# Big products of a slot put next to each other, dummy products in one group, a weight conversion tied to its place

## The chip, the cores and the metric

The kernel runs on one core of a Trainium2 chip. The metric is the device time of one execution in microseconds (us), less is better. Two kernels are compared by the medians of several executions on the same chip.

## The reference

Three computations follow each other. A recurrent attention over 768 steps for 4 batches of 8 heads of size 40, then an MLP with SiLU (320 to 2048 and back), then a gated MLP (320 to 1536 twice, a sigmoid on one, their product, and back to 320). Everything is float32.

```python
for t in range(S):                       # attention, S = 768
    y[:, :, t] = einsum('bhd,bhde->bhe', rt, state)
    Sa = einsum('bhde,bhe->bhd', state, at)
    state_decay = state * wt[:, :, None, :] - einsum('bhd,bhe->bhde', Sa, bt)
    state = state_decay + einsum('bhd,bhe->bhde', vt, kt)
...
h = x @ w_in;  g = h * (1.0 / (1.0 + np.exp(-h)));  x = g @ w_out          # first MLP
gate = 1.0 / (1.0 + np.exp(-(x @ w_gate)));  val = x @ w_val               # second MLP
out = gate * val @ w_out2
```

## The kernel before

The recurrence is cut into chunks of 32 steps. One chunk of one batch is a *slot*; there are 24 chunks times 4 batches, so 96 slots with attention work, and the first MLP trails the attention by 16 slots. A loop over `n` issues slot after slot, and an order written out as a string sets what stands behind what inside a slot: one string for the slots below 16 (`NL`), one for the others. Each letter is a short step on TensorE (PE), and most have a copy on ScalarE (ACT) or VectorE (DVE) behind them:

- `u` (`c_u`, tile `ps_u`), `v` (`c_ut`, `ps_ut`, "u's transpose"), `R` (`c_rhs` of the next slot, `ps_r`), `q` (`c_pu`, `ps_lp`), `t` (`c_st`, `ps_t`), `p` (`prep`, tile `wt`, then copied to `ks` and `yl`), `y` (`c_y`, `ps_y`), `s` (`c_s`, `ps_s`, the last link of a slot's state), `z` (`z_fix`, `ps_z`, odd slots up to 13 alone). All of these are small: 8 or 16 products, 16 to 40 columns wide. `ps_s` needs `ks` from `prep` and `sr` from `u`.
- `lb` (`e_sys`) builds the triangular systems of a later chunk, in about every second slot. DVE inverts them in short steps (`ztmp`, `zh`).
- The digits `0` to `3` call `mlp`. From slot 16 on, `0` and `1` are the two halves of the first MLP's up-projection (`m1_up`, tile `hp`, 8 products of 256 columns each) and `2` and `3` the two halves of the down-projection of the hidden block before (`m1_down`, tiles `acc`, 6 products of 320 columns each). Below slot 16 there is no MLP work yet, and each digit issues 4 *dummy* products with the identity instead (`warm(4, 2)`, tile `acc_w`, 256 columns); their result is never read.

The order on PE is fixed: `in_turn` makes a step follow the last product issued. The order on the other engines is decided by a scheduler that works ahead of time, except where `tc.issue_after` ties an instruction: `behind()` gives the instructions inside it a place behind the last copy to `yl` of `prep` and the last multiplication of `c_y` issued so far. Instructions without a tie may be put wherever the scheduler thinks an engine has room.

The weights arrive as 64-bit floats. `conv_load` starts the load (tile `cvr`), `conv_do` makes float32 of it (tile `cvt`: ACT lines 694 and 695, DVE lines 696 and 697, GpSimd line 698), and a float32 value is then split into a high and a low half. For the first MLP this runs inside `behind()` (`wtick`). For the second MLP `conv2` (lines 985 to 989) does it, without a tie. Its results lie in memory that the attention frees at its end, but `cvr` and `cvt` do not, so the first few conversions can begin long before.

Of the kernel before, what the change touches and what calls it, by code (L numbers as in the profile page):

```python
# [8 lines left out]
F32 = mybir.dt.float32  # L9
# [4 lines left out]
ALU = mybir.AluOpType  # L14
# [22 lines left out]
def kernel(  # L37
    ctx, tc, ins, wkab, rv, vn, w_in, w_out, w_gate, w_val, w_out2, out
):
    nc = tc.nc  # L40
# [145 lines left out]
    CW = 320  # L186
# [118 lines left out]
    NL = 16  # L305

    def in_turn():
        return tc.issue_after(last_op[0].ins) if now[0] >= 0 else nullcontext()
# [81 lines left out]
    def behind():  # L390

        g = ExitStack()
        for x in last_q.values():
            g.enter_context(tc.issue_after(x.ins))
        return g
# [79 lines left out]
    def warm(n, w=1):  # L475

        if not n:
            return
        ps = pa.tile([128, DM], F32, tag="acc0", name="acc_w")
        for _ in range(n):  # L480
            last_op[0] = nc.tensor.matmul(  # L481
                ps[:, :128 * w], identr,
                identr.unsqueeze(1).to_broadcast([128, w, 128]), start=True, stop=True,
            )
# [187 lines left out]
    def conv_load(rows, n, src, mp, cw):  # L672
        if wide:
            raw = mp.tile([128, cw, 2], I32, tag="cvr", name="cvr", bufs=4)
            t = raw.rearrange("p a b -> p (a b)")[:, :2 * n]
        else:
            raw = mp.tile([128, cw], F32, tag="cvt", name="cvt", bufs=2 + 1)
            t = raw[:, :n]
        r0 = 0
        for x in src if isinstance(src, tuple) else (src,):  # L680
            nc.sync.dma_start(t[r0:r0 + x.shape[0]], x)
            r0 += x.shape[0]
        return raw

    def conv_do(raw, rows, n, mp, cw):

        if not wide:
            return raw[:rows, :n]
        t = mp.tile([128, cw], F32, tag="cvt", name="cvt")[:rows, :n]
        lo, hi = raw[:rows, :n, 0], raw[:rows, :n, 1]  # L690
        ti = t.bitcast(I32)


        nc.scalar.mul(t, hi.bitcast(F32), 2.0 ** -112)
        nc.scalar.activation(lo, lo.bitcast(U32), AF.Copy, bias=2.0 ** 23, scale=2.0 ** -29)
        nc.vector.tensor_scalar(ti, ti, 3, None, op0=ALU.logical_shift_left)  # L696
        nc.vector.scalar_tensor_tensor(ti, hi, -0x80000000, ti, op0=ALU.bitwise_and, op1=ALU.bitwise_or)  # L697
        nc.gpsimd.tensor_tensor(ti, ti, lo, op=ALU.add)  # L698
        return t
# [34 lines left out]
    def wneed(p):  # L734

        f = min((p + 1) * max(1, NF1 // 8), NF1)
        o, n = 0, 0
        while o < FF1 and o < 128 * f:
            w = min(CW, FF1 - o)
            n += 3 + (NF1 if o + w == FF1 else (o + w) // 128) - o // 128  # L740
            o += w
        return n
# [33 lines left out]
    def defer(k, f):  # L776
        late.setdefault(now[0] + k, []).append(f)
# [7 lines left out]
    def hi_run(f, a):  # L785
        with behind(), tc.high_priority(offset=300):
            f(*a)
# [59 lines left out]
    if True:  # L847
# [12 lines left out]
        for x, t in enumerate(when):  # L860
# [7 lines left out]
            if stream[x] == e_units(gi)[-1]:  # L868
                i0 = t + 2
                i1 = min(gi * 8 - 4, i0 + 7)  # L870
                hi = lambda f: lambda *a: hi_run(f, a)
# [21 lines left out]

        def mlp(n, which):
            m = (n - 8 - 8)
            if m < 0:
                with in_turn():
                    warm(4, 2)
            if NP1 < 8 and m % 8 >= NP1:
                return  # L900
            if m < 0:
                return
            kb, p = divmod(m, 8)
            if kb >= NJ:
                return
            mm = kb * NP1 + p

            with tc.issue_after((last_op[0] if 1 else rhs_i[max(0, min(n, NS - 1) - [0, 0, 0, 0][which])]).ins):
                if which in (0, 1):
                    m1_up(mm, which)  # L910
                elif mm > 0:
                    m1_down(mm - 1, which - 2)

        for n in range(NS + 8 + 8):
            now[0] = n
            if 8 + 8 <= n < 16 + 8:
                while wpos[0] < min(wneed(n - 8 - 8), len(wsteps)) + LW:
                    wtick()
            for f in late.pop(n, ()):
                f()  # L920
            if n < NS and n not in rhs_i:
                c_rhs(n)
            for o in ['cuRqz0tp1vys23l', 'zcq01uv23tpRysl'][n >= NL]:
                if o in '0123':
                    mlp(n, int(o))
                turn = in_turn() if o in 'uvqptRsyz' else nullcontext()
                turn.__enter__()
                if o == 'R' and n + 1 < NS and n + 1 not in rhs_i:
                    c_rhs(n + 1)
                if o == 'z' and n % 2 == 0 and 0 < n < NS - 2:  # L930
                    z_load(n + 2)
                for x in range(2):
                    if o == 'zs'[x] and n % 2 == [1, 1][x]:
                        z_fix(n + 2 - [1, 1][x], x)
                if o == 'c' and n % 2 and n + 3 < NS:
                    c_load(n + 3)
                if o == 'l' and n % 2 == 0 and 0 < n and n + 2 < NS:
                    r_load(n + 2, 0)
                if o == 'l' and n % 2 and 1 < n and n + 1 < NS:
                    r_load(n + 1, 1)  # L940
                if o == 'u' and n < NS:
                    c_u(n)
                if o == 't' and 0 <= n - 3 < NS - NB:
                    c_st(n - 3)
                if o == 'q' and 0 <= n - 1 < NS:
                    c_pu(n - 1)
                if o == 's' and n < NS:
                    c_s(n)
                if o == 'v' and n < NS:
                    c_ut(n)  # L950
                if o == 'p' and n < NS:
                    prep(n)
                if o == 'y' and 0 <= n - 1 < NS:
                    c_y(n - 1)
                turn.__exit__(None, None, None)
            if 0 <= n - 1 < NS:
                defer(1, lambda n=n: x_store(n - 1))
                defer(5, lambda n=n: x_load(n - 1))
                defer(7, lambda n=n: x_split(n - 1))
            with gate(2), tc.high_priority(offset=-0):  # L960
                for f in ahead.get(n, ()):
                    f()
            with gate(1), tc.high_priority(offset=-0):
                w_ = len(wsteps) + LW
                need = w_ * (n + 1) // (8 + 8 + 3)
                while wpos[0] < min(need, w_):
                    wtick()
# [16 lines left out]

    def conv2(tmp, src, n, hi, lo):

        w = conv_do(conv_load(128, n, src, tmp, CW), 128, n, tmp, CW)
        nc.scalar.copy(hi, w)
        nc.vector.tensor_tensor(lo, w[:lo.shape[0]], hi[:lo.shape[0]].bitcast(F32), op=ALU.subtract)  # L989

    def w2_conv(pool, tmp, x):
        f0, f1 = fc[x], min(fc[x] + 512, FF2)
# [331 lines left out]
```

## Time and profile before

| | |
|---|---|
| runs shown, median of 3 | 1383.0 us (1380.85 to 1384.84) |
| the profiled execution | 1393.2 us, span 1391.5 us |
| PE busy | 1320.8 us (95%) |
| DVE, ACT, GpSimd busy | 798.0, 609.5, 275.5 us |
| mean granted TensorE clock | 0.91 of full speed |

The span is what lies between the first and the last instruction. Busy time is an average over stages: set-up to 58 us, slots without MLP to 272 us, slots with MLP to 907 us, then the end of the first MLP and the second MLP. [...]

### The profile page before, as it was taken

To read this page: it belongs to the slowest core of one execution; us is meant where nothing else is said; L and a number is where in the kernel's file an instruction comes from. 1 tells how busy PE (TensorE), PEld (TensorE's weight loads), DVE (VectorE), ACT (ScalarE), POOL (GpSimd) and SP (SyncE) were. 2 spreads that over 40 slices of the span, in tenths; PEclk is the share of its full clock that TensorE was granted. 3 is DMA by queue.
4 is the path that set the end of the run, shared out by engine and by line. 5 is a ranking of instruction groups with operands and counts; after the bars stand their busy time and mean duration, and the time that the engine had idled before them with its cause. 6 is when DMAs were issued, how large, how long until landed. Compare 5 with 4: busy or idle time off the path is not lost. (4 is left out here: it accounts for less than half of the span.)

```text
span 1391.5 us, 43139 instructions
## 1 busy us (share of the span) xinstructions
PE 1320.8 (95%) x17921; PEld 1205.1 (87%) x17921; DVE 798.0 (57%) x2094; ACT 609.5 (44%) x1392; POOL 275.5 (20%) x357
## 2 busy tenths in 40 slices
PE   3699999996999999999999999999999999999996
PEld 3688888986999999999999999998888888888885
DVE  6345376594869687877869573367883222232321
ACT  4124443553545555455554555567652222222221
POOL 5124344441122222222121100023320000000000
PEclk9855555598899999999999999999999999999998
DMA  7655455568566667666576534134640000000000
GB/s 197 155 130 143 117 150 119 156 148 174 127 139 151 148 164 150 149 159 150 149 163 159 128 84 108 31 120 123 206 129 19 20 19 19 20 0 20 3 17 22
DMA packets 222510, 152.55 MB, mean 110 GB/s; under 512 B 131570, under 2 KB 179058, under 8 KB 222306
## 3 DMA queue, kind: packets, MB, share of 16 engines
q1 hardware_dynamic: 222306, 149.71, 43.9%
q8 instruction: 143, 2.34, 0.7%
q14 instruction: 61, 0.50, 0.1%
HBM read 106.59 MB, written 42.72 MB: 107 GB/s over the span
## 5 line engine op out<-in xcount | busy, mean ns | idle before, releaser
L632 PE MATMUL hp<-X,w 120*128 120x256 f32 x1536 | 213.2, 293 | 0.0
L632 PEld LDWEIGHTS hp<-X,w 120*128 120x128 f32 x1536 | 195.5, 196 | 3.4
L1099 DVE TENSOR_TENSOR sg<-hv,sg 128x512 f32<-128x512 f32 x72 | 49.7, 690 | 186.1 <-PE hv L1091 161.5
L1091 PE MATMUL hg<-XT,wgv 128*128 128x512 f32 x576 | 151.2, 394 | 0.5 <-ACT x L663 0.5
L1091 PE MATMUL hv<-XT,wgv 128*128 128x512 f32 x576 | 147.2, 394 | 0.0
L641 ACT ACTIVATE hp<-hp 128x512 f32<-128x512 f32 x96 | 55.9, 582 | 205.4 <-PE hp L632 205.4
L246 POOL TENSOR_TENSOR et<-et 40x256 f32<-40x256 f32 x82 | 77.2, 941 | 330.5 <-DVE ztmp L355 70.3
L654 PE MATMUL acc<-o1h,gh 128*128 128x320 f32 x384 | 126.0, 328 | 2.6 <-ACT gh L642 2.5
L1091 PEld LDWEIGHTS hv<-XT,wgv 128*128 128x128 f32 x576 | 107.3, 188 | 23.5
L1091 PEld LDWEIGHTS hg<-XT,wgv 128*128 128x128 f32 x576 | 105.9, 188 | 21.4 <-ACT x L663 0.8
L575 DVE TENSOR_TENSOR stg<-ps_y,xt 40x128 f32<-40x128 f32 x192 | 54.9, 286 | 116.1 <-PE ps_y L567 111.9
L656 PE MATMUL acc<-o1h,gl 128*128 128x320 f32 x384 | 119.8, 312 | 1.2 <-DVE gl L643 1.2
L655 PE MATMUL acc<-o1l,gh 128*128 128x320 f32 x384 | 119.1, 310 | 0.0
L643 DVE TENSOR_TENSOR gl<-hp,gh 128x512 fp32r<-128x512 f32 x96 | 65.8, 686 | 89.8 <-ACT gh L642 87.0
L698 POOL TENSOR_TENSOR cvt<-cvt,cvr 128x256 int32<-128x256 int32 (+3 forms) x85 | 73.2, 864 | 160.8 <-DVE cvt L697 65.9
L359 DVE TENSOR_TENSOR zh<-zh,ztmp 128x126 f32<-128x126 f32 (+22 forms) x310 | 98.4, 317 | 7.3
L355 DVE TENSOR_TENSOR ztmp<-zh,z 128x126 f32<-128x126 f32 (+22 forms) x310 | 98.7, 318 | 6.8 <-DMA z<-sN 1.1
L1100 ACT CAST gh<-sg 128x512 fp32r<-128x512 f32 x72 | 44.6, 620 | 124.2 <-DVE sg L1099 124.2
L1098 ACT ACTIVATE sg<-hg 128x512 f32<-128x512 f32 x72 | 42.9, 596 | 121.9 <-PE hg L1091 121.8
L481 PE MATMUL acc_w<-identr 128*128 128x256 f32 x312 | 87.7, 437 | 1.0
L1111 PE MATMUL a<-o,gh 128*128 128x320 f32 x288 | 87.9, 309 | 0.4 <-DVE o L989 0.4
L1110 PE MATMUL a<-o,gh 128*128 128x320 f32 x288 | 87.5, 310 | 0.0
(183 smaller groups left out, 2656.1 us busy)
## 6 DMA issues: line engine op xcount, KB each, us to landing
xt<-sE SPq DMA_DIRECT2D x48, 322.5 KB
sE<-et SPq DMA_DIRECT2D x84, 161.2 KB
et<-in_wkab_dram SPq DMA_DIRECT2D x40, 258.0 KB
cvr<-in_moe_w_out_dram SPq DMA_DIRECT2D x28, 320.0 KB
et<-in_wkab_dram SPq DMA_DIRECT2D x40, 193.5 KB
sZ<-z SPq DMA_DIRECT2D x44, 128.0 KB
z<-sN SPq DMA_DIRECT2D x20, 256.0 KB
cvr<-in_moe_w_in_dram SPq DMA_DIRECT2D x42, 100.0 KB
```

The costliest lines, as they stand in the source:

```text
L246: (nc.vector if jj == 0 and i < 1 else nc.gpsimd).tensor_tensor(av, av, wc[r, :, :, 0:C], op=ALU.mult)
L355: nc.vector.tensor_tensor(tv, z[:, 0:rows, s:s + 1].to_broadcast([128, rows, m]), nt[:, s:s + 1, s + 1:].to_broadcast([128, rows, m]), op= ...
L359: last_inv[0] = nc.vector.tensor_tensor(z[:, 0:rows, s + 1:], z[:, 0:rows, s + 1:], tv, op=ALU.add)
L481: last_op[0] = nc.tensor.matmul(ps[:, :128 * w], identr, identr.unsqueeze(1).to_broadcast([128, w, 128]), start=True, stop=True,)
L632: last_op[0] = nc.tensor.matmul(hp[:, half, :], w1[0:rows, wi_, f * 128:(f + 1) * 128], X[xi][0:rows], start=(pi == 0), stop=(pi == 7),)
L654: nc.tensor.matmul(acc_t[c], a, o1(0, f), start=(f == 0), stop=False)
L655: nc.tensor.matmul(acc_t[c], a, o1(1, f), start=False, stop=False)
L656: last_op[0] = nc.tensor.matmul(acc_t[c], gl[:, fi, 128 * c:128 * c + 128], o1(0, f), start=False, stop=(f == NF1 - 1))
L698: nc.gpsimd.tensor_tensor(ti, ti, lo, op=ALU.add)
L1091: nc.tensor.matmul(hp, wgv[mi][f // 4][0:rows, wi_, f % 4 * 128:f % 4 * 128 + 128], X[0:rows, xi, :], start=(pi == 0), stop=(pi == 7))
L1110: nc.tensor.matmul(acc2_t[t], a, o2[0][f], start=(f == 0), stop=False)
L1111: nc.tensor.matmul(acc2_t[t], a, o2[1][f], start=False, stop=False)
```

## The change

Three edits. In slots 0 to 15 the 16 dummy products, issued in four places (4 behind `q`/`z`, 4 behind `p`, 8 behind `s`), become 24 in one place, behind `s`. In slots with MLP the order string changes, so that the two halves of the down-projection follow the two halves of the up-projection directly, and `u` and `v` come behind them. In `conv2` the load stays where it was, and everything behind it moves into `behind()`.

```diff
         def mlp(n, which):
             m = (n - 8 - 8)
-            if m < 0:
+            if m < 0 and which == 3:
                 with in_turn():
-                    warm(4, 2)
+                    warm(24, 2)
...
-            for o in ['cuRqz0tp1vys23l', 'zcq01uv23tpRysl'][n >= NL]:
+            for o in ['cuRqz0tp1vys23l', 'zcq0123uvtpRysl'][n >= NL]:
...
     def conv2(tmp, src, n, hi, lo):
 
-        w = conv_do(conv_load(128, n, src, tmp, CW), 128, n, tmp, CW)
-        nc.scalar.copy(hi, w)
-        nc.vector.tensor_tensor(lo, w[:lo.shape[0]], hi[:lo.shape[0]].bitcast(F32), op=ALU.subtract)
+        raw = conv_load(128, n, src, tmp, CW)
+        with behind():
+            w = conv_do(raw, 128, n, tmp, CW)
+            nc.scalar.copy(hi, w)
+            nc.vector.tensor_tensor(lo, w[:lo.shape[0]], hi[:lo.shape[0]].bitcast(F32), op=ALU.subtract)
```

The rows below give line, operation, output and inputs, the size of one output and how many follow each other.

On PE, slot 14 (one without `z`), before:

```order
L507 MATMUL ps_u<-rb0f,zs1f 32x40 x8
L490 MATMUL ps_r<-sr_179,xt_166 32x40 x8
L553 MATMUL ps_lp<-yr_168,vu 32x32 x16
L481 MATMUL acc_w<-identr 128x256 x4
L533 MATMUL ps_t<-ident,sr_179 40x40 x8
L466 MATMUL wt<-ident,xt_166 64x40 x8
L481 MATMUL acc_w<-identr 128x256 x4
L542 MATMUL ps_ut<-ident,sr_179 40x32 x8
L567 MATMUL ps_y<-yr_168,yl_182 40x32 x8
L518 MATMUL ps_s<-sr_179,ks_184 40x40 x8
L481 MATMUL acc_w<-identr 128x256 x8
```

The same slot on PE in the changed kernel:

```order
L507 MATMUL ps_u<-rb0f,zs1f 32x40 x8
L490 MATMUL ps_r<-sr_179,xt_166 32x40 x8
L553 MATMUL ps_lp<-yr_168,vu 32x32 x16
L533 MATMUL ps_t<-ident,sr_179 40x40 x8
L466 MATMUL wt<-ident,xt_166 64x40 x8
L542 MATMUL ps_ut<-ident,sr_179 40x32 x8
L567 MATMUL ps_y<-yr_168,yl_182 40x32 x8
L518 MATMUL ps_s<-sr_179,ks_184 40x40 x8
L481 MATMUL acc_w<-identr 128x256 x24
```

The two groups of 4 are gone from between the small steps, and the group behind `ps_s` has grown from 8 to 24.

On PE, the end of the up-projection in slot 18, before:

```order
L632 MATMUL hp<-X,w_158 128x256 x16
L507 MATMUL ps_u<-rb0r,zs1r 32x40 x8
L544 MATMUL ps_ut<-zs1r,rb0r 40x32 x8
L654 MATMUL acc_3893<-o1h_2486,gh 128x320
L655 MATMUL acc_3893<-o1l_2488,gh 128x320
```

In the changed kernel, the last rows of a down-projection of the same stage and what stands behind them:

```order
L655 MATMUL acc_3960<-o1l_2538,gh 128x320
L656 MATMUL acc_3960<-o1h_2536,gl 128x320
L507 MATMUL ps_u<-rb0r,zs0r 32x40 x8
L544 MATMUL ps_ut<-zs0r,rb0r 40x32 x8
L533 MATMUL ps_t<-ident,sr_179 40x40 x8
L466 MATMUL wt<-ident,xt_166 64x40 x8
```

`ps_u` and `ps_ut` have moved from ahead of the 12 products into `acc` to behind them; the rest keeps its order.

On ACT, slot 21, before (lines 694 and 695 on `128x256` are the first conversions of the second MLP):

```order
L508 ACTIVATE sr_179<-ps_u 32x320
L545 ACTIVATE vu<-ps_ut 40x256
L642 CAST gh<-hp 128x512
L694 ACTIVATE cvt<-cvr 128x256
L695 ACTIVATE cvr<-cvr 128x256
L534 COPY yl_182<-ps_t 40x320
L694 ACTIVATE cvt<-cvr 128x256
L695 ACTIVATE cvr<-cvr 128x256
L469 COPY ks_184<-wt 64x320
L470 COPY yl_181<-wt 64x320
```

And the same place on ACT in the changed kernel:

```order
L642 CAST gh<-hp 128x512
L508 ACTIVATE sr_179<-ps_u 32x320
L545 ACTIVATE vu<-ps_ut 40x256
L534 COPY yl_182<-ps_t 40x320
L469 COPY ks_184<-wt 64x320
L470 COPY yl_181<-wt 64x320
L492 CAST rb0r<-ps_r 32x320
L497 CAST rb0r<-ps_r 32x320
```

The conversions have left the slot (and slots 22 and 23, which held four more instructions of line 695), and the cast to `gh` now stands ahead of the copies of `ps_u` and `ps_ut`.

## Rows read from the trace of the kernel before

**Rows 1.** The page's second part: granted clock in 40 slices, in tenths.
```profile
PEclk9855555598899999999999999999999999999998
```

**Rows 2.** Stretches: us, engines' busy time, clock, DMA share, GB/s.
```profile
58.10:276.60 218.50, 217.02 (x3053) 193.32 (x3054) 109.56 (x314) 88.73 (x222) 82.58 (x100) 0.50 0.54 135
276.60:355.10 78.50, 63.28 (x1110) 59.11 (x1110) 54.05 (x161) 34.57 (x86) 23.28 (x32) 0.85 0.66 152
355.10:907.00 551.90, 548.41 (x10817) 516.61 (x10818) 395.28 (x1154) 293.51 (x689) 102.65 (x137) 1.00 0.59 135
907.00:977.00 70.00, 65.77 (x520) 62.94 (x520) 49.38 (x106) 49.68 (x122) 22.22 (x30) 1.00 0.40 122
```

**Rows 3.** Timeline of PE, slots without MLP: start, length, line, operation, count.
```profile
158.39 2.50 PE L481 MATMUL acc_w<-identr 128*128 128x256 f32 x8
160.82 1.27 PE L507 MATMUL ps_u<-rb0f,zs0f 96*32 96x40 f32 x16
161.90 1.27 PE L490 MATMUL ps_r<-sr,xt 96*32 96x40 f32 x16
163.10 1.07 PE L553 MATMUL ps_lp<-yr,vu 64*32 64x32 f32 x32
164.09 1.22 PE L481 MATMUL acc_w<-identr 128*128 128x256 f32 x4
165.25 0.72 PE L533 MATMUL ps_t<-ident,sr 40*40 40x40 f32 x8
```

**Rows 4.** Timeline of PE: the last step of slots 0, 15 and 16.
```profile
65.01 0.76 PE L518 MATMUL ps_s<-sr,ks 128*40 128x40 f32 x16
...
258.59 0.74 PE L518 MATMUL ps_s<-sr,ks 128*40 128x40 f32 x16
...
272.13 0.74 PE L518 MATMUL ps_s<-sr,ks 128*40 128x40 f32 x16
```

**Rows 5.** Timeline of PE, parts of the 56 dummies of the set-up; their durations.
```profile
48.63 1.70 PE L481 MATMUL acc_w<-identr 128*128 128x256 f32 x7
...
52.78 1.48 PE L481 MATMUL acc_w<-identr 128*128 128x256 f32 x11
...
L481 PE MATMUL acc_w<-identr x312: 278/415/583, 45.5 to 261.4; 128*128 128x256 f32 x156
```

**Rows 6.** Timeline of PE, a slot with MLP.
```profile
486.45 2.18 PE L632 MATMUL hp<-X,w 120*128 120x256 f32 x16
...
491.64 0.76 PE L490 MATMUL ps_r<-sr,xt 96*32 96x40 f32 x16
492.33 0.50 PE L567 MATMUL ps_y<-yr,yl 128*40 128x32 f32 x16
...
494.12 0.69 PE L553 MATMUL ps_lp<-yr,vu 64*32 64x32 f32 x32
494.75 2.18 PE L632 MATMUL hp<-X,w 120*128 120x256 f32 x16
```

**Rows 7.** Short stretches around changes of the clock, columns as in rows 2.
```profile
54.70:58.10 3.40, 3.40 (x101) 3.06 (x100) 0.42 (x1) 0.36 (x1) 1.40 (x4) 1.00 0.61 180
279.98:283.40 3.42, 3.01 (x88) 2.58 (x85) 3.27 (x8) 2.60 (x8) 2.40 (x4) 1.00 0.76 195
320.90:331.20 10.30, 7.24 (x99) 6.99 (x100) 5.80 (x16) 3.28 (x9) 3.95 (x7) 0.50 0.72 137
344.80:355.00 10.20, 6.25 (x92) 6.05 (x93) 4.79 (x18) 2.73 (x7) 0.66 (x1) 0.50 0.43 93
```

**Rows 8.** Waits of PE from 58 us on: total us, times, longest.
```profile
PE ps_s L518 <- ACT ks L469: 10.5, 2, 5.6
PE ps_u L507 <- DVE rb1r L498: 6.3, 12, 2.0
```

**Rows 9.** Timeline of ACT: the conversions that wait in slots 21 and 23.
```profile
321.75 0.43 ACT L694 ACTIVATE cvt<-cvr 128x256 f32<-128x256 f32 x1 [3.12 <-DMA cvr<-in_moe_w_gate_dram]
...
346.86 0.43 ACT L695 ACTIVATE cvr<-cvr 128x256 int32<-128x256 uint32 x1 [4.12 <-DMA cvr<-in_moe_w_val_dram]
```

## The prediction

> **What bounds the kernel now.** First the page's slices: the granted clock is in the nineties almost everywhere, but 5 tenths over seven slices near the start [rows 1]. The stretches then say what goes with it. From 58.1 to 276.6 us PE is busy 217.0 of 218.5 us at clock 0.50, while DVE, ACT and GpSimd are busy 110, 89 and 83 us and the transfers hold 0.54 of their engines [rows 2]. [...] From 276.6 to 355.1 us PE is idle for 15.2 of 78.5 us, with a clock of 0.85. From 355.1 to 907 us PE idles 3.5 of 551.9 us at 1.00: what is moved there has little idle time to win. The list of waits names what the idle time was for: 10.5 us in two waits of `ps_s` for `ks`, 6.3 us in twelve of `ps_u` for `rb1r` [rows 8].
>
> **Dummies in one group.** Fifteen slots pass between the last steps of slots 0 and 15: (258.59 - 65.01)/15 = 12.9 us each [rows 4]. The 8 dummies take 2.43 us to the next step, a group of 4 takes 1.16 [rows 3]; together 4.75 us a slot, which leaves 8.15 us of small products.
>
> [...] `R` goes from 1.20 us [rows 3] to 0.69 [rows 6], `ps_lp` from 0.99 to 0.63; together 1.32/2.19 = 0.60. So 8.15 becomes 4.9 us. A dummy takes (1.70 - 0.415)/6 = 0.214 us at the low clock and (1.48 - 0.28)/10 = 0.12 at the high one [rows 5]; 24 are 5.1 or 2.9 us. At the high clock a slot is 4.9 + 2.9 + 0.1 = 7.9 us, 5.0 less than now, 75 us in 15 slots. At the low clock it is 8.15 + 5.3 = 13.45 us, 0.55 more than now, 9 us in all 16 slots.
>
> Does the clock rise? The 56 dummies of the set-up began at 45.5 us at the low spacing and had the high one by 52.8 [rows 5]; the groups of 8 and 4 among small products never raised it in 218 us [rows 2, 3]. One group of 24 lasts 5.1 us at the low clock, twice the longest group now. I take it that it raises the clock in nearly every slot in which it begins low, late in the group.
>
> Does it stay up? After the set-up's dummies there were only small products, `ps_z` and `lb` among them; the clock held to 58.1 us and then fell, with PE busy throughout [rows 7, 2]. In the MLP stage a stretch of small products alone (279.98 to 283.40, PE 3.0 us busy) passed at 1.00 and the clock stayed [rows 7]. The slots without MLP hold `ps_z` only up to slot 13, between other steps, so I side with the second row, though not for slots that also wait.
>
> [...]
>
> Waits come with it. A shorter slot leaves less time to DVE (110 us in 17 slots, 6.5 a slot) and ACT (5.2), both below 7.9, and the transfers, 0.54 of 12.9 us, are 7.0 us a slot. So nothing forbids 7.9 us, but little is spare, and `ps_s` no longer has four dummies between it and the copy to `ks`. Bounds from rows: below, 15.2 - 10.5 = 4.7 us of other idle time in the some 8.5 slots of the next stage, 0.55 us a slot; above, the longest wait of `ps_u`, 2.0 us, in each slot [rows 2, 8]. I take 1.0, as weights are converted in both stages: 15 us. And I take the clock to fall in one slot of three, for the rest of the slot and most of the next group: half of the small work, 2.45 us, takes 4.1, and some 16 of 24 dummies cost 0.094 us more each, together 3.1 us, 15 us for five falls. Left: 75 - 15 - 15 = **-45 us** (bounds -67 without falls and with 0.55 us of wait, -22 with 2.0 us and a fall in most slots).
>
> **Slot 16** now takes 272.13 - 258.59 = 13.5 us at the low clock [rows 4]. A later slot with `lb` and a down-projection takes 494.75 - 486.45 = 8.3 [rows 6], and slot 16 has no down-projection. Less a wait of 1 us, **-4 us** (0 to -5).
>
> **The conversion tied.** In slots 21 and 23 ACT stands 3.12 and 4.12 us in front of a conversion whose weights have not arrived [rows 9]; the copies to `yl` and `ks` are queued behind it, and `ps_s` waits for `ks` [rows 8]. In the order of the changed kernel the conversions are gone from there; the copies follow their products. That is 10.5 us. Each stall is followed by a stretch of clock 0.50, with 7.24 and 6.25 us of PE work in it [rows 7], of which 0.40 goes at the high clock: 5.4 us. Sum **-16 us** (the low end, -10, if one of the two stalls finds another cause). What is late next: the four raw buffers stay full until the attention ends, and two finished conversions with two half finished ones, some 2.5 us of ACT (six instructions of 0.43 us [rows 9]), now run after 907 us, where ACT is busy 49.7 of 70 us and PE idles 4.2 [rows 2]. Nothing excludes that they hide (0), nothing excludes 3; **+1.5 us**.
>
> **Big products next to each other.** `ps_u` waited for `rb1r`, 6.3 us in all [rows 8]; the 12 products into `acc`, which need data of the slot before, now lie ahead of it and cover that: **-6 us**. Each slot changes neighbours on PE: one switch from small to big products goes, one is moved. Rows 2 put all idle time there at 3.5 us, so I count it at 0, with 5 us to either side. The cost that is not visible: the copies of `ps_u` and `ps_ut` (0.43 us each, as the other copies of rows 9) now come just ahead of those to `yl` and `ks`. From `ps_u` to `ps_s` there are still `ps_ut`, `ps_t`, `wt`, `ps_r` and `ps_y`, some 2 us, for four copies of 0.43 us, 1.7 us. It fits, narrowly; kept at 0, up to +10 us.
>
> **Sum.** -45 - 4 - 16 + 1.5 - 6 = -69.5. Against the profiled execution, 1393.2 us, that is 1323.7. That execution lies 10 us above the median of the runs shown, 1383.0; the change is measured against those, so I predict 1383 - 69 = **1314 us**.
>
> **Rivals.**
> *The clock rises and falls in each slot.* Then a slot has some 16 dummies at the low clock and 8 at the high one (4.5 us), and 2.4 us of high clock left for the small work, which does 4.0 us of it: 4.5 + 2.4 + 4.15 = 11.05 us, 1.85 less than now, -28 us; less a wait here and there, and with -4 becoming -2, about -45 in all: 1338. For it: the fall after the set-up's dummies. Against it: the small-only stretch at 1.00 [rows 7].
> *DVE, ACT or the transfers become the bound* in these slots, as 7.0 us a slot of transfers on average means some slots of 9 or more. With slots of 10.5 us, -36 in place of -45: 1323 to 1335, inside the range.
> *The group of 24 doesn't raise the clock*, and the change does not do there what it is shaped for. For it: 218 us of a busy PE at 0.50. Against it: the set-up's group. It gives +9 in the early slots, -16 + 1.5 - 6 elsewhere, -11.5: 1371.
> *Slower: the run of small products in the MLP slots becomes too long.* `ps_u` and `ps_ut` join it, so that in the some 40 slots with `lb` it lasts over 4 us instead of 3.5. If the clock fell there, each fall would cost as those after the two stalls did, 0.40 of 6 to 7 us, 2.7 us, and up to 4 us if the stretch of 10.2 us is filled with work. From some 20 falls at 3.5 us the gain of 70 is gone; with one in each of the 79 slots the kernel takes some 1383 + 206 = 1590, with one in each slot with `lb` 1454. Against it: the moved products are busy ones, the waits go, and rows 2 show 552 us at 1.00 with runs nearly as long.
>
> **How the numbers follow.** Clock mostly high in the early slots: 0.62 (own range 1286 to 1330). Rising and falling, or bound by another engine: 0.25 (1323 to 1350). Never raised: 0.07 (1371). Too long a run of small products: 0.04; other new waits that eat all: 0.02. The range 1286 to 1350 leaves out some 0.06 below and 0.14 above. No change from measurement means within 0.3%, 4 us: faster 0.92, same 0.02, slower 0.06.
>
> **What the next profile would show.** If right: the page's slices read 9 from the third on, a slot below 16 takes 8 to 10 us, `ps_s` no longer waits 5 us for `ks`, no line 694 in the middle of the attention. If the clock rises and falls: fives and nines in turn, with slots of 11 us. If a rival engine binds: clock high, PE idle several us a slot with one releaser on top. Wrong altogether would be a clock below 1.00 between 355 and 907 us, or a new wait of PE at the start of the second MLP of more than 5 us.

## The result

The changed kernel takes 1329.97 us (median of 4 runs, 1327.21 to 1334.88). The kernel before, run beside it on the same chip, takes 1383.92 us (median of 4, 1380.85 to 1391.84). The ratio is 0.9606, with a 95% interval of 0.9556 to 0.9656: 54 us less. The forecast was 1314 us, with a range of 1286 to 1350. The time lies in the range, 16 us above the forecast and at the edge of the likeliest case's own range (1286 to 1330).

The profiled execution took 1334.88 us, 5 us above the median, with a span of 1333.1 us. So the two profiled spans differ by 58.4 us, and that is the number that the stretches below must add up to. The profiled execution of the kernel before was a slow one, 9 us above the median, while the ratios in this document are taken from fast executions alone.

First the page of the changed kernel, its line of granted clocks in 40 slices, to be read beside [rows 1]:

```profile
PEclk9887878989999999999999999999999999999998
```

The seven slices of 5 are gone, but what stands in their place is not a row of nines either: the early slices read 7 to 9. The next view, stretches of the changed kernel with busy time of PE, weight loads, DVE, ACT and GpSimd, then clock, transfer share and GB/s, answers to [rows 2]:

```profile
61.20:224.60 163.40, 145.77 (x2881) 137.65 (x2880) 114.36 (x290) 76.94 (x195) 77.31 (x92) 0.81 0.67 166
224.60:308.00 83.40, 78.58 (x1436) 75.37 (x1435) 63.46 (x185) 45.61 (x111) 30.69 (x40) 0.89 0.64 158
308.00:863.00 555.00, 552.88 (x10897) 532.86 (x10893) 397.69 (x1172) 300.38 (x705) 106.91 (x142) 0.99 0.59 138
863.00:918.60 55.60, 51.18 (x366) 47.88 (x365) 41.48 (x91) 42.11 (x105) 19.10 (x24) 1.00 0.46 136
```

The first row is slots 0 to 15, from last step to last step. Before, PE had 1.5 us of idle time in 218.5 [rows 2]. Now it idles 17.6 us in 163.4, and the transfers hold 0.67 of their engines in place of 0.54. The third row reads 0.99: somewhere in the slots with MLP the clock now falls for a moment.

To see where the 58.4 us came from, the same marks are taken in both kernels: the last step `ps_s` of slots 0, 15, 16, 24 and 91, and the first product of the second MLP. The timeline of PE of the changed kernel, start and length first, has them at

```profile
61.17 0.56 PE L518 MATMUL ps_s<-sr,ks 128*40 128x40 f32 x10
...
224.61 0.43 PE L518 MATMUL ps_s<-sr,ks 128*40 128x40 f32 x6
...
236.75 0.43 PE L518 MATMUL ps_s<-sr,ks 128*40 128x40 f32 x12 [0.40 <-ACT ks L469]
...
307.99 0.48 PE L518 MATMUL ps_s<-sr,ks 128*40 128x40 f32 x16
...
820.86 0.48 PE L518 MATMUL ps_s<-sr,ks 128*40 128x40 f32 x16
...
918.63 0.74 PE L1093 MATMUL hg<-XT,wgv 128*128 128x512 f32 x2 [0.53 <-ACT x L663]
```

and the kernel before, beside the marks in [rows 4], at

```profile
359.70 0.48 PE L518 MATMUL ps_s<-sr,ks 128*40 128x40 f32 x16
...
879.47 0.48 PE L518 MATMUL ps_s<-sr,ks 128*40 128x40 f32 x16
...
977.08 1.19 PE L1091 MATMUL hg<-XT,wgv 128*128 128x512 f32 x4 [0.53 <-ACT x L663]
```

| stretch | before, us | after, us | difference | the forecast's term |
|---|---|---|---|---|
| up to `ps_s` of slot 0 | 65.0 | 61.2 | -3.8 | none |
| slots 0 to 15 | 193.6 (12.9 a slot) | 163.4 (10.9) | -30.2 | -45 |
| slot 16 | 13.5 | 12.1 | -1.4 | -4 |
| slots 17 to 24 | 87.6 | 71.2 | -16.4 | -16 |
| slots 25 to 91 | 519.8 | 512.9 | -6.9 | -6 |
| slot 92 to the second MLP | 97.6 | 97.8 | +0.2 | +1.5 |
| second MLP | 414.4 | 414.5 | 0 | 0 |

One row is off by much: the early slots gave 30 us and not 45. The first row was not in the sum at all. The 8 dummies that stood ahead of the first `ps_s` are gone, 2.4 us at the spacing of [rows 3]. But with these dummies in place, the runs with the order and the conversion alone (below) had that mark at 62.8 and 61.8 us, so most of the 3.8 us can also be a difference between executions.

The early slots themselves, in the timeline of PE of the changed kernel (groups of dummies, and what begins the slot behind each):

```profile
119.94 4.62 PE L481 MATMUL acc_w<-identr 128*128 128x256 f32 x24
124.50 0.76 PE L507 MATMUL ps_u<-rb0f,zs1f 96*32 96x40 f32 x16
...
128.24 3.13 PE L481 MATMUL acc_w<-identr 128*128 128x256 f32 x24
...
132.35 0.76 PE L507 MATMUL ps_u<-rb1f,zs1f 96*32 96x40 f32 x16
...
138.07 4.24 PE L481 MATMUL acc_w<-identr 128*128 128x256 f32 x24
142.24 0.76 PE L507 MATMUL ps_u<-rb0f,zs0f 96*32 96x40 f32 x16
...
145.98 3.14 PE L481 MATMUL acc_w<-identr 128*128 128x256 f32 x24
```

The same 24 products take 3.13 us in one slot and 4.2 to 4.6 in the next. From 61.2 to 224.6 us the clock was at 0.50 in twelve stretches, 61 us in all, and at 1.00 between them, as the mean of 0.81 says too (2 x 0.19 x 163.4 = 62). Each of the twelve ended inside a group of dummies. Each began among small products, or in the first 0.6 us of the group behind them, and that group took longer for it (4.62 us at 119.94, where the clock was at 0.50 to 123.5).

The list of waits of PE in the changed kernel from 50 us on (total, times, longest) answers to [rows 8]:

```profile
PE ps_y L567 <- DVE yr L556: 7.5, 4, 2.7
PE ps_z L444 <- DVE ln L284: 4.7, 2, 3.2
PE ps_u L507 <- DVE rb1r L498: 4.1, 1, 4.1
PE ps_lp L553 <- DVE stg L575: 2.2, 3, 1.0
...
PE ps_s L518 <- ACT ks L469: 0.4, 1, 0.4
```

`ps_s` waits 0.4 us for `ks`, and not 10.5. `ps_u` waits once for `rb1r`, and not twelve times. In their place stand waits for DVE in the early slots, and one stall of 4.13 us in slot 18. The timeline of DVE ahead of that stall:

```profile
251.80 0.29 DVE L229 TENSOR_SCALAR wcl<-et 112x256 f32<-112x256 f32 x1 [2.79 <-DMA et<-in_wkab_dram]
...
261.07 0.47 DVE L498 TENSOR_TENSOR rb1r<-ps_r,rb1r 32x320 fp32r<-32x320 f32 x1
```

DVE stood 2.79 us for a load of `et`. From then on it was busy for 9.4 of 9.6 us, with scans and inversion steps among other work, ahead of the subtraction for `rb1r`, which came at 261.07; `ps_u` followed at 261.69. What the late load and what the order on DVE has in the stall wasn't separated. The clock was at 0.50 from 260.1 to 273.7 us.

### The profile page after: what moved, and what is told of

Its sections match the earlier page's. It is cut to its first block, busy times and chain, and to the rows that moved or that the text cites. A ratio compares the mean times of both kernels' runs of the same rounds, so it can differ in the third digit from the quotient of the medians.

```text
span 1333.1 us, 43363 instructions
## 1 busy us (share of the span) xinstructions
PE 1257.6 (94%) x18049; PEld 1168.8 (88%) x18049; DVE 806.7 (61%) x2094; ACT 609.8 (46%) x1392; POOL 278.7 (21%) x357
## 5 line engine op out<-in xcount | busy, mean ns | idle before, releaser
L654 PE MATMUL acc<-o1h,gh 128*128 128x320 f32 x384 | 119.8, 312 | 2.5 <-ACT gh L642 1.7
L355 DVE TENSOR_TENSOR ztmp<-zh,z 128x126 f32<-128x126 f32 (+22 forms) x310 | 99.0, 319 | 11.6 <-DMA z<-sN 5.7
L1112 PE MATMUL a<-o,gh 128*128 128x320 f32 x288 | 87.6, 310 | 0.2 <-ACT gh L1102 0.2
L1114 PE MATMUL a<-o,gl 128*128 128x320 f32 x288 | 78.7, 310 | 0.5 <-DVE gl L1103 0.5
```

The costliest lines, as they stand in the source:

```text
L355: nc.vector.tensor_tensor(tv, z[:, 0:rows, s:s + 1].to_broadcast([128, rows, m]), nt[:, s:s + 1, s + 1:].to_broadcast([128, rows, m]), op= ...
L654: nc.tensor.matmul(acc_t[c], a, o1(0, f), start=(f == 0), stop=False)
L1112: nc.tensor.matmul(acc2_t[t], a, o2[0][f], start=(f == 0), stop=False)
L1114: nc.tensor.matmul(acc2_t[t], gl[:, 128 * t:128 * t + 128], o2[0][f], start=False, stop=(f == NF2 - 1))
```

## Experiments

In all of these, "slots 0 to 15" is the time between the same two marks as above.

### One edit at a time

Each part alone on the kernel before.

```diff
# only_group: the kernel before with
-            if m < 0:
+            if m < 0 and which == 3:
                 with in_turn():
-                    warm(4, 2)
+                    warm(24, 2)
# only_order: the kernel before with
-            for o in ['cuRqz0tp1vys23l', 'zcq01uv23tpRysl'][n >= NL]:
+            for o in ['cuRqz0tp1vys23l', 'zcq0123uvtpRysl'][n >= NL]:
# only_conv: the kernel before with conv2's part behind the load in behind()
```

> The kernel before with the dummies' edit alone (24 in one group behind ps_s in slots 0 to 15). If the early slots' gain is the clock's and independent of the other two edits: slots 0 to 15 take some 10.9 us as in the changed kernel instead of 12.9, clock up and down in turn, the two waits of ps_s for ks in slots 19 to 24 stay; about 1352 us (-31). If the three edits need each other (the early slots gain because the conversions are gone, or the stalls of slots 16 to 24 went because the early slots changed): clearly off from that, 1365 or more, or 1340 or less.

> The kernel before with the order string alone. If big products next to each other cover the wait of ps_u for rb1r and little else: slots from 24 on lose 0.1 us each and the steps of 7.55 and 7.65 us, about -7 us between slots 24 and 91, less some 5 us for one or two new falls of the clock; 1377 us (-7). If the longer run of small products costs more than it brings: 1384 or more. If it also removes the stalls of slots 16 to 24: 1365.

> The kernel before with the conversion tied alone. If the two 5 us waits of ps_s for ks come from conversions ahead of the copies on ACT: both waits go, with the two stretches of clock 0.50 behind them, slots 16 to 24 lose some 16 us, 1368 us (-16). If those waits came from something else (the copies themselves, transfers): they stay and the time is 1383.

Measured on one chip, where the kernel before took 1382.8 us:

| | median, us (range) | ratio, 95% interval | slots 0 to 15 | 17 to 24 | 25 to 91 |
|---|---|---|---|---|---|
| only_group | 1340.58 (1339.44 to 1341.48) | 0.9692 [0.9644, 0.974] | 162.8 | 72.9 | 519.5 |
| only_order | 1368.72 (1365.62 to 1373.34) | 0.9898 [0.9859, 0.9938] | 187.7 | 83.1 | 508.2 |
| only_conv | 1373.22 (1351.84 to 1378.98) | 0.9843 [0.9788, 0.9897] | 187.6 | 71.4 | 519.1 |

The group alone gives 43 of the 54 us, by its ratio; the forecast for it, 1352 us, took the two stalls of `ps_s` to stay, and they didn't. The order alone takes 11.6 us from slots 25 to 91, where neither of the others takes more than 0.7; that term is the order's. The tied conversion takes 16.2 us from slots 17 to 24, what the forecast gave it. But the order shortens those slots too, by 4.5 us, and the group by 14.7, and here the parts overlap: alone they give 43, 14 and 22 us by the ratios, some 78 together, and all three give 54. Of these, the 22 is the least certain: the executions with the conversion alone scatter over 27 us, and the interval allows 14 to 29. The waits tell why the parts overlap. PE in the run with the conversion alone:

```profile
PE ps_u L507 <- DVE rb1r L498: 6.4, 13, 2.1
...
PE ps_s L518 <- ACT ks L469: 0.6, 2, 0.4
```

and in the run with the group alone:

```profile
PE ps_u L507 <- DVE rb1r L498: 10.6, 13, 5.5
...
PE ps_s L518 <- ACT ks L469: 0.8, 2, 0.4
```

The waits of `ps_u` for `rb1r` stay in both, thirteen of them; only the order removes them. The two stalls of `ps_s` for `ks` of [rows 8] are gone in both. With the order alone the wait for `ks` is short as well (0.6 us), but the stalls haven't gone: they have moved to `ps_r`, which waits 5.9 us in three for `sr`, the copy of `ps_u`. ACT and PE of that run, at one of the three:

```profile
311.24 0.84 ACT L695 ACTIVATE cvr<-cvr 128x256 int32<-128x256 uint32 x2 [2.10 <-DMA cvr<-in_moe_w_gate_dram]
312.11 0.42 ACT L508 ACTIVATE sr<-ps_u 32x320 f32<-32x320 f32 x1
...
312.59 0.76 PE L490 MATMUL ps_r<-sr,xt 96*32 96x40 f32 x16 [2.32 <-ACT sr L508]
```

Another conversion in that run waits 3.06 us for `w_val`, and `ps_r` behind it 2.24. With only the group, the conversions still stand in the middle of the attention too, but ACT waits for their weights at most 1.69 us (where [rows 9] had 3.12 and 4.12), and no stall comes of it. So in these runs an untied conversion of the second MLP stalled PE where ACT stood 2.10 to 4.12 us for its weights, and not where it stood at most 1.69 us; with the tie, the first of them on ACT comes only behind slot 91, in every run that has it. What the tie adds on top of the two other edits wasn't run.

The 6 us that the runs with the order and the conversion alone gained in slots 0 to 15 can't be put to either edit: neither moves a product there. In both, the clock was up for some 17 us near 100 us (a mean of 0.55 over these slots), with the old groups of dummies in place. Single executions of the kernel before, beside these runs, differ too: 1370 to 1392 us.

### The place and the size of the group

spread24 gives the 24 dummies of a slot back to the old places, 6, 6 and 12; group16 and group12 make the one group smaller; group0 has no dummies in the slots at all; split24_8 adds 8 between `wt` and `ps_ut`.

```diff
# spread24, the rest as in the changed kernel
-            if m < 0 and which == 3:
+            if m < 0:
                 with in_turn():
-                    warm(24, 2)
+                    warm(6, 2)
# group16, group12, group0
-                    warm(24, 2)
+                    warm(16, 2)      # 12; 0
# split24_8
-            if m < 0 and which == 3:
+            if m < 0 and which in (1, 3):
                 with in_turn():
-                    warm(24, 2)
+                    warm(24 if which == 3 else 8, 2)
```

> The changed kernel with its 24 dummies a slot at the places of the kernel before (6, 6 and 12). If a long group is what raises the clock: clock 0.50 through slots 0 to 15 as in the kernel before, slots of 14.6 us (12.9 and 8 dummies of 0.214 us more), 1330 + 15 x 3.7 = 1386 us. If the number of dummies in a slot is what counts: as the changed kernel, 1330 us. In between if groups of 12 raise it in some slots.

> The changed kernel with 16 dummies in its group, the number of the kernel before. If one group is what raises the clock, whatever the total: up and down as in the changed kernel, slots shorter by 8 x 0.12 to 0.21, 1.0 to 1.7 us where PE is the bound: 1310 us. If it needs the larger number: clock 0.50 through slots 0 to 15, slots of 8.15 + 3.6 + some wait = 12 us, 1330 + 15 x 1.1 = 1347 us.

> The changed kernel with 12 dummies in its group, the longest group of the spread run. If a group of 12 raises the clock by itself: as spread, less 12 dummies, 1310 us. If in the spread run the groups of 6 had a part in it: clock 0.50, slots of 8.15 + 2.7 + 0.5 = 11.4 us, 1330 + 15 x 0.5 = 1337 us.

> The changed kernel without any dummy in slots 0 to 15. PE has only small products there: clock 0.50 throughout, 8.15 us of work a slot and the waits. If PE at the low clock is all that bounds: 8.2 to 9 us a slot against 10.9, 1330 - 15 x 2.2 = 1297 us. If DVE and the transfers bound at about the pace of the changed kernel (they were the releasers of its waits): 10 to 11 us a slot, 1320 to 1332 us; slot 16 begins at the low clock either way, some 3 us lost.

> The changed kernel with 8 more dummies in each of slots 0 to 15, between prep and u's transpose. If the clock falls in odd slots because of their long run of small products with ps_z: that run is broken, the falls in slots without a wait of PE go, and 3 us for each of some 7 falls come back against 16 x 1.0 us more dummies: 1325 us. If the falls follow the waits of PE for DVE: they stay, and the 8 dummies cost 16 us or more: 1347 us.

spread24 was measured beside the single edits; the other four ran together on one chip, where the kernel before took 1389.26 us. PE busy and clock are those of slots 0 to 15 in each profile, idle is the rest.

| | dummies a slot | median, us (range) | ratio, 95% interval | slots 0 to 15, us | clock | PE busy | PE idle |
|---|---|---|---|---|---|---|---|
| before | 16 | 1383.92 (1380.85 to 1391.84) | | 193.6 | 0.50 | 192.7 | 0.9 |
| spread24 | 24 | 1334.45 (1332.87 to 1342.48) | 0.9664 [0.9612, 0.9717] | 164.8 | 0.83 | 153.5 | 11.3 |
| split24_8 | 32 | 1330.32 (1328.36 to 1332.47) | 0.960 [0.9528, 0.9672] | 163.9 | 0.90 | 151.5 | 12.4 |
| changed kernel | 24 | 1329.97 (1327.21 to 1334.88) | 0.9606 [0.9556, 0.9656] | 163.4 | 0.81 | 145.8 | 17.6 |
| group16 | 16 | 1331.16 (1328.68 to 1337.4) | 0.9595 [0.9522, 0.9668] | 163.9 | 0.79 | 134.1 | 29.8 |
| group12 | 12 | 1336.81 (1333.74 to 1340.0) | 0.9635 [0.9561, 0.9708] | 162.5 | 0.71 | 134.4 | 28.1 |
| group0 | 0 | 1323.13 (1320.5 to 1324.78) | 0.954 [0.9468, 0.9611] | 159.0 | 0.50 | 125.3 | 33.8 |

Read the last two columns downward from spread24. PE's work falls by 28 us to group0, and PE's idle time grows by 22.5. The sum stays at 159 to 165 us, with the clock anywhere between 0.50 and 0.90. Once PE is not full any more, something else sets the early slots, at 10.6 to 11 us each, and what the clock saves on PE comes back as a wait. One group in place of several is not what matters either: with the same 24 dummies, spread24 is as short there as the changed kernel. Of the cases laid out beforehand, 1330 us for spread24 (if the number of dummies counts) and 1320 to 1332 for group0 came about. For group16 and group12 the clock rose, and the 1310 us forecast for that case didn't follow (group12 landed at the other case's 1337, without its clock of 0.50 throughout). In split24_8 most of the falls went (four stretches at 0.50 in place of twelve), also without a gain.

The kernel without dummies has the lowest median of these. Its runs lie below those of split24_8 on the same chip (1324.78 at most against 1328.36 at least). Against the changed kernel it was only compared through the kernel before; those intervals overlap. Between the two profiled spans lie 11.3 us, of which 4.4 are in slots 0 to 15; slots 25 to 91, where the changed kernel's clock fell twice, have 4.5 of the rest. The stretch of its early slots:

```profile
62.10:221.10 159.00, 125.25 (x2523) 115.64 (x2522) 109.86 (x290) 77.51 (x197) 78.36 (x93) 0.50 0.70 172
```

Its PE work is what the forecast had for the small products at the low clock, 125.25/15 = 8.35 us a slot against 8.15. PE idles a fifth of these slots (33.8 of 159.0 us), their mean granted clock is 0.50, and the kernel has the lowest median of the series, 1323.13 us.

### What holds the early slots

Three engines and the transfers came into question. These runs leave work out, one suspect each, on the kernel without dummies; thin24 does the same with the 24 dummies.

```diff
# thin0 (without dummies) and thin24 (with 24): conv_do for the first MLP's weights
         nc.scalar.mul(t, hi.bitcast(F32), 2.0 ** -112)
+        if thin:
+            return t
# noinv0 (without dummies): inv_steps
-        for s in range(s0, s1):
+        for s in range(s0 if gi == 0 or gi > 2 else s1 - 1, s1):
# load4: thin0, with a quarter of the columns of the first MLP's weights loaded
-            nc.sync.dma_start(t[r0:r0 + x.shape[0]], x)
+            nc.sync.dma_start(t[r0:r0 + x.shape[0]], x[:, :2 * (n // part)] if part > 1 else x)
...
-                raw_t[k] = conv_load(rows, n, src, mp, CW)
+                raw_t[k] = conv_load(rows, n, src, mp, CW, part=4)
```

> The changed kernel without dummies, and with the conversion of the first MLP's weights cut to its first ACT instruction (line 695, DVE lines 696 and 697 and GpSimd line 698 are left out there, so the first MLP computes with wrong weights); the loads stay. Without dummies slots 0 to 15 took 159.0 us with PE busy 125.3. If the chain of conversions through ACT, DVE and GpSimd is what they wait for, its 27 us of DVE and 26 us of GpSimd go and the slots come down to 128 to 140 us. If the transfers bind them (share 0.70), they stay at 154 to 160. If DVE's inversions do, 145 to 155.

> The changed kernel with its 24 dummies and the same conversion left out as in the run without dummies. If the conversions are what holds the early slots, and the clock pays once they are gone, slots 0 to 15 take 120 to 135 us (8 to 9 us each, the forecast's own figure), at or below the same kernel without dummies. If the clock doesn't pay, they take as long as or longer than without dummies, 140 to 160 us. If the transfers bind, 158 to 165 as now.

> The changed kernel without dummies, and with the inversion of the second and third chunk group cut to the last step of each portion (the systems come out wrong): some 36 us of DVE go from slots 0 to 15, conversions and transfers stay. If DVE's queue behind the inversions holds these slots, 159.0 us comes down to 130 to 145. If the conversion chain or the transfers hold them, 152 to 160.

> The run thin0 (no dummies, conversion cut to one ACT instruction; slots 0 to 15 took 155.0 us with PE busy 124.8 and a transfer share of 0.71), and of the first MLP's weights only a quarter of the columns is loaded and used four times over (wrong weights again): some 6.8 of the 27.8 MB that are moved in these slots go. If the transfers are what holds the early slots at some 155 us once PE has less to do, they come down to 130 to 145 us; PE's own work of 124.8 us is the floor. If they don't, and what is left are the steps' waits for each other (PE for a copy on ACT or DVE and back), the slots stay at 150 to 157 us with the share at some 0.55.

The stretches of slots 0 to 15, with columns as in the first such view above. Conversion cut (thin0):

```profile
63.30:218.30 155.00, 124.61 (x2522) 115.54 (x2522) 81.79 (x234) 64.97 (x169) 50.31 (x65) 0.50 0.71 177
```

Inversions cut (noinv0):

```profile
63.40:218.90 155.50, 124.63 (x2523) 115.60 (x2522) 82.03 (x210) 76.68 (x197) 77.59 (x93) 0.50 0.72 174
```

Conversion cut, with 24 dummies (thin24):

```profile
59.60:216.70 157.10, 141.72 (x2883) 133.86 (x2882) 83.45 (x234) 65.26 (x169) 50.66 (x65) 0.85 0.70 175
```

Conversion cut and a quarter of the weights loaded (load4):

```profile
64.20:206.00 141.80, 124.20 (x2521) 115.40 (x2522) 80.93 (x234) 65.22 (x169) 50.65 (x65) 0.50 0.63 146
```

DVE lost 28 us in thin0 and noinv0 each, GpSimd 28 in thin0, and the slots lost 4.0 and 3.5 us. So without dummies neither the conversions' arithmetic nor the inversions are, by themselves, what holds them, and my first reading, that DVE's queue binds (in the changed kernel 70% busy and named by most waits), fell with it for that kernel; the two weren't left out together. Dummies and a clock of 0.85 made the slots no shorter than in thin0 (157.1 us), as the theory that the clock doesn't pay had it. When 7 of 27 MB were not moved, with as many instructions on all engines, 13.2 us went, to 141.8, as the case for the transfers had it: PE's idle time fell from 30.4 to 17.6 us. The whole kernels took 1319.56 us (thin0, 1316.19 to 1322.93), 1322.27 (thin24, 1321.86 to 1322.67), 1326.37 (noinv0, 1322.67 to 1330.06) and 1308.9 (load4, 1307.98 to 1309.82), two runs each, with ratios to the kernel before of 0.9592 [0.9358, 0.9825], 0.9611 [0.9403, 0.982], 0.9641 [0.9402, 0.988] and 0.9469 [0.9391, 0.9548]. These intervals overlap, so the comparison of the four rests on the stretch of one profiled execution each, and for thin0 and load4 also on runs that don't overlap, though on two chips.

How a load of weights holds up the attention can be seen in one slot. In the timeline of ACT of the kernel without dummies, slot 6:

```profile
117.94 0.49 ACT L695 ACTIVATE cvr<-cvr 128x320 int32<-128x320 uint32 x1 [4.06 <-DMA cvr<-in_moe_w_out_dram]
118.33 0.36 ACT L545 ACTIVATE vu<-ps_ut 40x256 f32<-40x256 f32 x1
118.60 0.34 ACT L445 COPY zs1f<-ps_z 16x256 f32<-16x256 f32 x1
```

A conversion at the head of ACT's queue waits 4.06 us for weights that haven't landed. Behind it stand the copies of `ps_ut` and of `ps_z` into `zs1f`, whose products had ended on PE at 112.0 and 113.7 us. On PE of the same kernel:

```profile
113.62 0.76 PE L518 MATMUL ps_s<-sr,ks 128*40 128x40 f32 x16
119.00 1.27 PE L507 MATMUL ps_u<-rb0f,zs1f 96*32 96x40 f32 x16 [4.62 <-ACT zs1f L445]
```

With the conversion cut (thin0), ACT waits 1.63 us for a load at this place and `ps_u` 1.67. With a quarter of the weights to load as well (load4), it reads

```profile
113.05 0.76 PE L518 MATMUL ps_s<-sr,ks 128*40 128x40 f32 x16
113.88 1.27 PE L507 MATMUL ps_u<-rb0f,zs1f 96*32 96x40 f32 x16
```

The list of waits would name ACT as the culprit for `ps_u`. One step further back it is a transfer: the three rows of ACT have 4.06 us of waiting for a load in front of two copies that needed nothing of it.

For the changed kernel itself, with its dummies and a clock of 0.81, the trace names another queue. In slots 0 to 15 ACT waited for weights once, 3.1 us. Of PE's 17.6 us of idle time 15.7 are waits for DVE, and in seven of them, 13.5 us together, DVE was busy right up to the step that PE waited for, with inversions, conversions and the splitting of `X`. DVE and PE at one of the seven:

```profile
105.31 0.17 DVE L355 TENSOR_TENSOR ztmp<-z,zh 128x15 f32<-128x15 f32 x1
105.51 0.87 DVE L359 TENSOR_TENSOR z<-z,ztmp 128x15 f32<-128x15 f32 x1
106.41 0.42 DVE L556 TENSOR_TENSOR yr<-ps_lp,msk 64x256 f32<-64x256 f32 x1
...
100.08 0.70 PE L553 MATMUL ps_lp<-yr,vu 64*32 64x32 f32 x32 [0.63 <-DVE z L359]
...
106.89 0.75 PE L567 MATMUL ps_y<-yr,yl 128*40 128x32 f32 x16 [2.74 <-DVE yr L556]
```

`ps_lp` was done at 100.8 us, and the multiplication that makes `yr` of it came at 106.4. DVE had been busy without a break since 94.7, and had stood 3.9 us for a load of `et` before that. The inversions were not left out with the dummies in place, so DVE's queue is an untested candidate there.

Left open: 17.6 us of idle time remain in load4, spread over waits for several engines, of at most 3.7 us each, and it is not shown which share of the changed kernel's own 17.6 us is due to loads and which to the order on DVE. A version that converts the first MLP's weights one step later, so that each load has longer to land, follows from this and wasn't tried.

## Why the prediction was right, and which term was off

**What bounds the kernel.** Right for the kernel before: slots 0 to 15 were bound by PE at the low clock (busy 192.7 of 193.6 us, at 0.50). It stopped being true for the kernel after (145.8 of 163.4 us, at 0.81), and that is the point where the sum went wrong.

**Dummies in one group (-45 forecast, -30.2 measured).** This is the mis-sized term. Its pieces can be checked against the profile of the changed kernel, if each instruction of PE is put to the clock under which it ran. Small products and `lb` took some 19.6 us low and 64.0 high, dummies some 36.6 low and 25.6 high. With the forecast's ratios (0.60 for small products, 0.12/0.214 for dummies) all of it at the high clock would be 75.8 + 46.1 = 121.9 us, 8.1 a slot; the forecast had 7.9. Waits were 17.6 us; it had 15. The falls of the clock cost 145.8 - 121.9 = 23.9 us; it had 15, for five falls at 3.1 us each, where there were twelve stretches at 2.0. These three, +3.4, +2.6 and +8.9, make up the 15 us. The -30.2 itself is counted from the one profiled execution of the kernel before, 9 us above its median: against the 187.7 and 187.6 us that the runs with the order and the conversion alone took there, it is -24.

That is the bookkeeping, and it suggests that without the falls the slots would be 24 us shorter. The experiments say otherwise. From the changed kernel to group16 PE's work fell by 11.7 us, and the slots took 0.5 us longer. The step that failed is the one that took the waits as a fixed price, "1.0, as weights are converted in both stages: 15 us", added to PE's work. They are what is left over when the rest of these slots' work needs some 160 us, however long PE takes. Without dummies late loads are part of that rest, 13.2 us by load4; in the changed kernel it is argued from the waits alone that steps queued on DVE are. The forecast had one clue, the transfers' 7.0 us a slot and "little is spare", and used it for a rival and not in the sum.

**The rivals.** Two of them came about together. The clock did rise and fall, though not in each slot, with 10.9 us a slot against the 11.05 forecast for that. And something other than PE bounds the slots at 10.6 to 11 us, where the forecast had 10.5 and 1323 to 1335 us. The group did raise the clock, from 0.50 to 0.81, so the third didn't happen. That it could have stayed away at no loss, as group0 shows, no rival had.

**Slot 16 (-4, measured -1.4).** It ran at the low clock for 4.7 of its 12.1 us and ended with a wait of 0.4 us for `ks`. The term is small, and where a fall happens to lie decides it.

**The conversion tied (-16, measured -16.4).** The cause is right: `ps_s` no longer waits 5 us for `ks`, and with the conversion alone slots 17 to 24 lose 16.2 us. That the group alone lost the stalls too, by loads that came in time, the forecast didn't have. That the size holds with all three edits is in part luck. Before, the clock was low for 28.3 us of slots 17 to 24; afterwards for 13.7 us, all of it around the new stall in slot 18, which nobody had forecast and which itself cost 4.1 us. Set against this are waits of `ps_u` for `rb1r`, 3.9 us in these slots, which the forecast had counted in the next term. The +1.5 us at the start of the second MLP was +0.2.

**Big products next to each other (-6, measured -6.9).** The number is right and its makeup is not. Of the 6.3 us that `ps_u` waited for `rb1r` [rows 8], only 2.4 lay in slots 25 to 91. PE in these slots, in the kernel before and with the order alone, columns as before:

```profile
359.70:879.47 519.77, 516.40 (x10255) 486.60 (x10250) 382.40 (x1126) 274.32 (x643) 100.10 (x133) 1.00 0.62 142
345.88:854.12 508.24, 507.38 (x10254) 489.11 (x10250) 378.28 (x1126) 275.34 (x644) 99.67 (x133) 1.00 0.62 144
```

The order takes 11.5 us, and 2.5 of them are idle time. The other 9.0 are busy time of PE, over the same products at the same clock, 0.13 us a slot. Most of them lie where one step meets the next: before, the last product into `acc` took 0.24 us to the start of `ps_t` behind it, and now 0.15 to the start of `ps_u`; the first product into `acc` took 0.23 to the next behind `ps_ut`, and now 0.15 behind `hp`. Against that, the last product into `ps_ut` took 0.04 us to `acc` and now takes 0.12 to `ps_t`, which leaves 0.10 of the 0.13 us. This is the switch between big and small products that the forecast put at 0, "with 5 us to either side", because the stretch had little idle time. But 9.0 of the 11.5 us stood in busy time, and idle time doesn't show them.

The rival on the slower side, a fall of the clock behind a longer run of small products, came about twice in slots 25 to 91, at 502.4 and 690.1 us. In the slots with `lb` there, the run lasted 3.8 us before and 4.4 in the changed kernel, and 5.5 and 5.6 us in these two. Stretches of the changed kernel around the two, columns as before:

```profile
498.90:502.36 3.46, 2.50 (x98) 2.33 (x95) 3.24 (x12) 1.46 (x4) 0.00 (x0) 1.00 0.69 206
502.36:505.79 3.43, 3.43 (x36) 3.37 (x30) 3.29 (x12) 0.00 (x0) 0.00 (x0) 0.51 0.54 140
686.70:690.08 3.38, 2.42 (x82) 2.25 (x77) 3.22 (x11) 0.63 (x2) 0.00 (x0) 1.00 0.86 214
690.08:693.50 3.42, 3.42 (x18) 3.42 (x17) 3.33 (x14) 0.51 (x1) 0.13 (x1) 0.51 0.60 152
```

Each time there was a slot with `lb`, a wait of about 1 us among its small products (`ps_lp` for the multiplication at line 575), and then the big products ran at a clock of 0.51. The slot took 10.7 us in place of 8.2, so the two cost 5 us together. The order alone, split24_8 and group0 had no such fall there and took 507 to 508 us: without this the term is some -11.5. The six falls in slots 25 to 91 of the other runs with this order (spread24, group16, group12 and load4 one each, thin24 two) also came behind such a wait, of 0.89 to 1.19 us. Whether the wait is needed beside the run of small products wasn't tested. It stayed at two of the 27 slots with `lb` there; from slot 16 on there are 32 of them, and not "some 40".

**Predicted signs.** No line 694 in mid-attention for the second MLP's weights: right; the first pair of lines 694 and 695 on `128x256` comes at 848.2 us, in the last slot of the attention. Slices of 9 from the third on and slots of 8 to 10 us: wrong; sevens to nines in turn, and 10.9 us. A clock below 1.00 between 355 and 907 us, named as a sign of being wrong altogether, did show, in the two falls, and cost 5 us.

## What to carry to other kernels

When one engine is full and a change takes work from it, its waits are not a fixed price to be added: find the next chain's own time for the stage and take the larger of the two. Here the rest of the slots' work needed some 160 us, and everything that the clock could save beyond that was lost. Before work is added to keep a clock up, run the stage without that work: here no dummies at all did no worse than any arrangement of them. A stall that a scheduler's placement caused can vanish with a change nearby, or only change its name in the list of waits (10.5 us of `ps_s` for `ks` became 5.9 us of `ps_r` for `sr`), so look for what ended it and not for the name. And split a list of waits by stage before a term is taken from it: the 6.3 us held 2.4 for the stage that was to gain them.

## What the runs showed of the hardware that was not expected

The stage's time hardly depended on the granted clock: 159.0 us at 0.50 without dummies, 163.9 at 0.90 with 32 dummies a slot. And loads came late with the transfer engines' share at 0.70: in the kernel without dummies ACT stood up to 4.06 us for one, with copies queued behind it. Cutting the bytes by a quarter (27.4 to 20.7 MB in slots 0 to 15, thin0 against load4) took 13.2 of 155.0 us. With the order alone PE was busy 9.0 us less over 67 slots (507.4 in place of 516.4), at the same clock and with the same products.
